# Turning the q and k of two head pairs in one DMA transfer, with v on GpSimd's queue

## The chip, the cores and the metric

The kernel runs on one core of a Trainium2 chip. The time is device time in microseconds for one execution, the median of several runs. A profiled execution gives the busy times, waits and DMA packets that are read here. Its engines are called PE (TensorE, the matrix engine; PEld are its weight loads), DVE (VectorE), ACT (ScalarE), POOL (GpSimd) and SP (SyncE, which computes nothing here and only issues DMAs). SPq in a row means SP's queue.

## The reference

Attention with a softmax that has one extra term in its denominator, and then a feed-forward layer with mish:

```python
batch, n_heads, seq, head_dim = (8, 12, 448, 64)      # q, k, v, float32
scores = scale * np.matmul(q, k.transpose(0, 1, 3, 2))
m = np.max(scores, axis=-1, keepdims=True)
e = np.exp(scores - m)
attn = e / (np.sum(e, axis=-1, keepdims=True) + np.exp(-m) + 1e-09)
x = np.matmul(attn, v)          # then heads side by side: 3584 x 768
h = x @ w_in                    # 768 x 2048
g = h * np.tanh(np.log1p(np.exp(np.minimum(h, 20.0))))   # (h itself over 20)
out = g @ w_out                 # 2048 x 768
```

## The kernel before

**Tiling.** A head pair is two heads of one batch. There are 48 of them, six per batch, and a unit is three pairs, so there are 16 units with attention, numbered from 0. The first six pairs (units 0 and 1) run in an opening of their own. From unit 4 on (`GROUP_FROM = 12`, called grouped) all units have one shape, and that is where the change lies. "The sixth unit" is unit 5, with pairs 15, 16 and 17. The instructions run on each engine in the order in which the code writes them.

**One unit u.** It works on pairs p0, p0 + 1, p0 + 2, and nxt = p0 + 3 is the first pair of the next unit. It has two halves.

The attention half has 12 steps n. In each step ACT takes the exponentials of one score tile (L330), PE makes further scores (L293, L296, L301), DVE finds their maxima (L319), and PE fills in pieces of the second feed-forward product of an earlier batch (L511) and the weighted sums of the unit before (`av_pair`, L403). Between them stand the loads and casts of the next unit's pairs: at n = 0, 3 and 6 one pair is loaded, q, k and v in three DMAs on SP's queue (L148), and at n = 3 and 6 the pair that was loaded one slot earlier is cast to bf16 by GpSimd (q on L192 or L194, k on L198, v on L178). The third pair is cast at the start of the other half.

The feed-forward half has eight columns f = 0 to 7 of the first product with mish (`mm1_mish`, L422 on PE and L450 on ACT). In it the attention weights of the unit's three pairs are normalised (`normalise`, L366 on DVE for two pairs and L364 on GpSimd for the third), and each pair's weights are turned by one DMA transpose from SP (L370, `eT<-en`). At f = 7 stand the first scores of the next unit, which need the turned q and k of pair nxt.

**How q and k come to be turned.** Scores need q and k with the head dimension on the partitions. Two ways are in use. `transpose_pair` does it on PE: four transposes each for q and k (L215) into PSUM at f = 1, 3 or 5, and then `evac_qk` copies the result out, q scaled on DVE (L255) and k on ACT (L263). `turn_by_dma` does it by DMA transposes from SP's queue (L229, `qkT<-q_bf` and `qkT<-k_bf`), one for q and one for k. Which pairs go which way is in `TURN_BY_DMA`: of unit 5 and later the first pair of each unit (15, 18, and so on to 45), and pair 46. The first pair's turn is issued after step n = 8, and that of pair 46 after step 11. For a pair turned by DMA the scale is multiplied in when q is cast.

After either way, `rest_of` copies on GpSimd the columns of q that make up the last score tile (L237, L238). For pairs turned by DMA it stands at f = 3, ahead of GpSimd's share of the normalising.

**What orders the work.** SP's queue is served in order, and a DMA that waits for its data holds up all that stand behind it: loads, turns, eT transposes and stores (L476) share it. GpSimd also works in order. Its own DMA queue carries the weight loads (L174) until unit 4 and nothing afterwards.

Of the kernel before, what the change touches and what calls it, by code (L numbers as in the profile page):

```python
# [10 lines left out]
BF16 = mybir.dt.bfloat16  # L11
# [4 lines left out]
UNIT_PAIRS = 3  # L16
# [3 lines left out]
def kernel(  # L20
# [9 lines left out]
    nc = tc.nc  # L30

    B, H, S, D = q.shape
# [3 lines left out]
    NT = 4  # L36
    SP_ = S // NT
# [10 lines left out]
    N_PAIRS = B * HP  # L48
# [4 lines left out]
    def pool(name, bufs, space=None):  # L53
        if space is None:
            return ctx.enter_context(tc.tile_pool(name=name, bufs=bufs))
        return ctx.enter_context(tc.tile_pool(name=name, bufs=bufs, space=space))

    PS = bass.MemoryType.PSUM
    singles = pool("singles", 1)
    ld_pool = pool("ld", 4)  # L60
    bf_pool = pool("bf", 6)
    qk_pool = pool("qk", 3)
    st_pool = pool("st", 5)
    eT_pool = pool("eT", 3)
    xT_pool = pool("xT", 2)
# [16 lines left out]
    def banks_apart():  # L82
# [16 lines left out]
    w_in_sb = singles.tile([128, DM_T, d_ff], BF16)  # L99
    w_out_sb = singles.tile([128, FF_T, d_model], BF16)  # L100

    N_EN = 4
    en_bufs = [
        singles.tile([128, NT, NTILE, 128], BF16, tag=f"en{i}", name=f"en{i}")
        for i in range(N_EN)
    ]
# [4 lines left out]

    GROUP_FROM = 2 * HP
    ONE_COPY = range(1, HP + UNIT_PAIRS)
    TURN_BY_DMA = tuple(p for p in range(5 * UNIT_PAIRS, N_PAIRS) if p % UNIT_PAIRS == 0 or p == N_PAIRS - UNIT_PAIRS + 1)
    SCALED_IN_CAST = (*ONE_COPY, *TURN_BY_DMA)
    q_rests = [
        singles.tile([128, 2, 64], BF16, tag=f"qr{i}", name=f"qr{i}") for i in range(UNIT_PAIRS)
# [4 lines left out]
    loaded, casted, qkT, att, xT, gT, o_sbs, stats = {}, {}, {}, {}, {}, {}, {}, {}  # L122
# [16 lines left out]
    def load_pair(p, which="qkv"):  # L139
        if p >= N_PAIRS:  # L140
            return
        b, h0 = p // HP, (p % HP) * 2
        tiles = loaded.setdefault(p, [])
        for nm, src in (("q", q), ("k", k), ("v", v)):
            if nm not in which:
                continue
            t = ld_pool.tile([SP_, 2, NT * D], FP32, tag=f"{nm}_f", name=f"{nm}_f")
            nc.sync.dma_start(  # L148
                out=t, in_=src[b, h0 : h0 + 2].rearrange("h (p t) d -> p h (t d)", t=NT)
            )  # L150
            tiles.append(t)
# [28 lines left out]
    def cast_pair(p, with_v=True):  # L180
        if p >= N_PAIRS:
            return
        q_f, k_f = loaded[p][:2]
        q_bf = bf_pool.tile([SP_, NT, 2, D], BF16, tag="q_bf", name="q_bf")
        k_bf = bf_pool.tile([SP_, NT, 2, D], BF16, tag="k_bf", name="k_bf")
        v_bf = bf_pool.tile([SP_, 2, NT * D], BF16, tag="v_bf", name="v_bf", bufs=9)
        by_t = "p h (t d) -> p t h d"
        cast_q, cast_k = nc.gpsimd.tensor_copy, nc.gpsimd.tensor_copy
        if p == 0:
            cast_q, cast_k = nc.vector.tensor_copy, nc.scalar.copy  # L190
        if p not in SCALED_IN_CAST:
            cast_q(out=q_bf, in_=q_f.rearrange(by_t, t=NT))  # L192
        else:
            nc.gpsimd.tensor_scalar(  # L194
                out=q_bf, in0=q_f.rearrange(by_t, t=NT),
                scalar1=SCALE, scalar2=1.0, op0=ALU.mult, op1=ALU.mult,
            )
        cast_k(out=k_bf, in_=k_f.rearrange(by_t, t=NT))  # L198
        casted[p] = (q_bf, k_bf, v_bf)
        if with_v:  # L200
            cast_v(p)
# [20 lines left out]
            by_s = ps[:, :].bitcast(BF16).rearrange("p (s n) -> p s n", s=2)[:, :, 0:S]  # L222
        qkT[p] = (by_s, own)

    def turn_by_dma(p):
        qk = qk_pool.tile([128, 2, S], BF16, tag="qkT", name="qkT")
        pair = qk[:, 0, :], qk[:, 1, :]
        for dst, src in zip(pair, casted[p]):
            nc.sync.dma_start_transpose(  # L229
                out=dst.rearrange("c (t q) -> c t q", q=SP_),  # L230
                in_=src.rearrange("q t h d -> q (t h d)"),
            )
        qkT[p] = pair

    def rest_of(p):
        qT, q_rest = qkT[p][0], q_rests[p % UNIT_PAIRS]
# [3 lines left out]
    def evac_qk(p, act=False):  # L240
        if p >= N_PAIRS:
            return
        by_s, own = qkT[p]
        mo_free.extend(own)
        qk = qk_pool.tile([128, 2, S], BF16, tag="qkT", name="qkT")
        qT, kT = qkT[p] = qk[:, 0, :], qk[:, 1, :]
        if p in ONE_COPY:
            copy = nc.scalar.copy if act else nc.vector.tensor_copy
            copy(out=qk, in_=by_s)
            return  # L250
        q_ps, k_ps = by_s
        if act:
            nc.scalar.mul(qT, q_ps[:, 0:S], SCALE)
        else:
            nc.vector.tensor_scalar(  # L255
                out=qT, in0=q_ps[:, 0:S], scalar1=SCALE, scalar2=None, op0=ALU.mult
            )
        if p >= GROUP_FROM:
            rest_of(p)
        if p == 0 or own and not act:  # L260
            nc.vector.tensor_copy(out=kT, in_=k_ps[:, 0:S])
        else:
            nc.scalar.copy(kT, k_ps[:, 0:S])  # L263
# [10 lines left out]
    def scores(idx):  # L274

        p, s = divmod(idx, STEPS)
        if s == 0:
# [4 lines left out]
            att[p] = {nm: t[:, at, :] for nm, t in stats.items()}  # L282
            att[p].update(en=en_bufs[p % N_EN], whole=dict(stats))
        st = att[p]
# [303 lines left out]
    BY_POOL = 3  # L588
    LEAD = UNIT_PAIRS + 1
    LOAD_AT = (0, 3, 6)  # L590
    TURN_AFTER = (8, 11)
    LAST_AV_AT = 9
    HEAD = HP

# [63 lines left out]
    for u in range(UNITS_PER_B, N_UNITS + 2 * UNITS_PER_B):  # L658
# [5 lines left out]
        p0 = u * UNIT_PAIRS  # L664
        nxt = p0 + UNIT_PAIRS
# [5 lines left out]
        for n in range(steps):  # L671
            pi, s = divmod(n, STEPS)
            p, idx = p0 + pi, p0 * STEPS + n
            late_tp = u == UNITS_PER_B and n == STEPS
            if late_tp:
                transpose_pair(p0 + 2)
            exps(idx)
            if grouped:
                flush_late()
                for what, arg in (GROUPED_LATE_AV if u == LATE_AV else GROUPED)[n]:  # L680
                    if what == "fill":
                        for _ in range(min(arg, len(filler))):
                            fn, w = filler.popleft()
                            fn()
                            done += w
                    elif what in ("av0", "av1"):
                        bank = sc_banks[int(what[2])][0]
                        av_pair(p0 - UNIT_PAIRS + arg, bank=bank)
                    else:
                        flush_late()  # L690
                        for i in arg:
                            scores(p0 * STEPS + i)
                if n in LOAD_AT:
                    at = p0 + LOAD_AT.index(n)
                    if u > first_mm2:
                        load_pair(at + LEAD - 1)
                        if n:
                            cast_pair(at + LEAD - 2)
                    elif n < LOAD_AT[-1]:
                        load_pair(at + LEAD)  # L700
                        cast_pair(at + LEAD - 1)
                if u - UNITS_PER_B < len(W_AT):
                    load_w(W_AT[u - UNITS_PER_B].get(n, 0))
                if n in TURN_AFTER and nxt + TURN_AFTER.index(n) in TURN_BY_DMA:
                    turn_by_dma(nxt + TURN_AFTER.index(n))
                continue
            if late_tp:
                evac_qk(p0 + 2, act=True)
            if u == UNITS_PER_B + 1:
                for i, part in enumerate(TURN_AT[1].get(n, [])):  # L710
                    turn_on_pe(*part)
                    if n == 0:
                        mm1_ahead(0, FIRST_AHEAD[i])
            flush_late()
            acc += weight[n]
            want = int(total * acc / sum(weight) + 1e-6)
            while done < want:
                fn, w = filler.popleft()
                fn()
                done += w  # L720
            scores_ahead(end)
            if n in LOAD_AT:
                load_pair(p0 + LOAD_AT.index(n) + LEAD)
                cast_pair(p0 + LOAD_AT.index(n) + LEAD - 1)
            if u - UNITS_PER_B < len(AV_AT):
                early = AV_AT[u - UNITS_PER_B]
                if n in early:
                    av_pair(early[n], act=early[n] in AV_BY_ACT)
                if u == UNITS_PER_B:
                    for part in TURN_AT[0].get(n, []):  # L730
                        turn_on_pe(*part, act=part in TURN_BY_ACT)
            elif u == N_UNITS and n == LAST_AV_AT:
                for i in range(UNIT_PAIRS):
                    av_pair(p0 - UNIT_PAIRS + i, bank=sc_banks[i][0])
            if u - UNITS_PER_B < len(W_AT):
                load_w(W_AT[u - UNITS_PER_B].get(n, 0))
# [9 lines left out]
        for f in range(FF_U):  # L746
# [3 lines left out]
            if moe:  # L750
                first = to_group and nxt == GROUP_FROM
                bank, ff = sc_banks[0][0] if f == 1 else None, w * FF_U + f
                if to_group:
                    at = (FIRST_MISH_BANK if first else MISH_BANK)[f]
# [68 lines left out]
```

## Time and profile before

| | |
|---|---|
| median of 3 runs | 463.99 us (462.11 to 465.33) |
| the profiled execution | 462.06 us, of which the span from its first to its last instruction is 460.3 us |
| granted PE clock over the span | 0.993 |
| busy PE, DVE, ACT, POOL | 430.8, 342.3, 343.3, 186.6 us |
| DMA issues for q, k, v | 48 each, 224 KB each, on SP |
| DMA transposes on SP | 43 of eT, 12 of q, 12 of k |

A row of a timeline gives the start in us from the span's start, the duration in us, the engine, line and operation, what it writes and reads, how many instructions were merged into the row, and in brackets how long the engine had been idle before and what ended that. In a row of a group of instructions, the counts and the durations in ns (smallest, median, largest) stand together. Durations on SP are those of the issue; the landing of the data is told apart.

### The profile page before, as it was taken

Reading aid. Unit: us, or ns where it says so; the run is one execution under the profiler, and the core shown is the slowest. Engines: PE = TensorE matmul, PEld = TensorE weight load, DVE = VectorE, ACT = ScalarE, POOL = GpSimd, SP = SyncE. Lnnn points to the kernel's source line nnn. Section 1 sums busy time; section 2 is a strip of 40 time slices with the busy share of each in tenths; the row PEclk is TensorE's granted clock in tenths of the full one; section 3 lists DMA queues with packets and bytes.
Section 4 is the critical chain, followed back from the end, with each engine's and each line's share of the span. In section 5 each row is a group of like instructions: output and inputs, shape, how many; then the busy total and the mean of one; then the engine's idle time right before and its main releaser. Section 6 shows DMA issues by size and latency. Waiting matters only on the chain.

```text
span 460.3 us, 8676 instructions
## 1 busy us (share of the span) xinstructions
PE 430.8 (94%) x2952; PEld 229.0 (50%) x2952; DVE 342.3 (74%) x718; ACT 343.3 (75%) x906; POOL 186.6 (41%) x352
## 2 busy tenths in 40 slices
PE   4586798899998999999999999999999989999997
PEld 2243445444444554545455555545454545555565
DVE  4899968879796988889787988889887969421121
ACT  5998988989795969788897969696988879211300
POOL 4666839254418172625444271707254450000000
PEclk9997999999999999999999999999999999999999
DMA  8999999999999999999999999999999996950213
GB/s 218 221 194 229 272 190 229 207 210 197 215 254 240 223 221 227 252 216 264 204 248 215 253 197 244 199 234 249 209 243 201 258 198 142 182 127 0 70 34 104
DMA packets 213900, 93.11 MB, mean 202 GB/s; under 512 B 170592, under 2 KB 210400, under 8 KB 213856
## 3 DMA queue, kind: packets, MB, share of 16 engines
q1 hardware_dynamic: 206272, 86.22, 89.2%
q0 software_dynamic: 7488, 6.29, 9.4%
q8 instruction: 23, 0.38, 0.3%
q14 instruction: 21, 0.17, 0.1%
q10 hardware_dynamic: 96, 0.05, 0.0%
HBM read 45.61 MB, written 11.01 MB: 123 GB/s over the span
## 4 chain that ended last, share of the span: by engine, by line
PE 72%; DMA 8%; ACT 6%; DVE 6%; issue 2%; SPq 2%; POOL 1%; POOLq 0%; DVEq 0%
PE mo L511 29%; PE mo L422 21%; PE b L403 6%; PE b L422 6%; ACT en L330 5%; DVE negm L319 4%; PE b L293 3%; DMA k_f<-in_k_dram 3%; DMA q_f<-in_q_dram 2%; PE sc L293 2%; DMA eT<-en 2%; DMA qkT<-k_bf 1%; SPq L370 1%; PE mo L301 1%; PE sc L215 1%
## 5 line engine op out<-in xcount | busy, mean ns | idle before, releaser
L511 PE MATMUL mo<-w_out_sb,gT 128*128 128x384 bf16 (+1 forms) x896 | 141.5, 304 | 0.9 <-DVE o_sb L498 0.7
L422 PE MATMUL mo<-xT,w_in_sb 128*128 128x448 bf16 x600 | 124.3, 353 | 0.8 <-DVE xT L412 0.3
L511 PEld LDWEIGHTS <-gT 128*128 128x128 bf16 x896 | 80.2, 98 | 58.8 <-issue 20.2
L422 PEld LDWEIGHTS <-w_in_sb 128*128 128x128 bf16 x768 | 72.2, 98 | 66.6 <-issue 7.2
L450 ACT ACTIVATE gT<-mo 128x448 bf16<-128x448 f32 x98 | 53.0, 544 | 70.0 <-PE mo L422 69.5
L330 ACT ACTIVATE en<-sc,negm 128x448 bf16<-128x448 f32 x156 | 97.8, 641 | 7.6 <-DVE negm L319 6.3
L319 DVE TENSOR_REDUCE negm<-b 128x1 f32<-128x448 f32 x144 | 79.8, 617 | 19.4 <-PE b L296 19.4
L330 ACT ACTIVATE en<-b,negm 128x448 bf16<-128x448 f32 x144 | 89.7, 652 | 0.8 <-DVE negm L319 0.8
L319 DVE TENSOR_REDUCE negm<-sc 128x2 f32<-128x896 f32 x84 | 84.2, 1016 | 6.3 <-PE sc L296 4.0
L364 POOL TENSOR_SCALAR en<-en,rden 128x448 bf16<-128x448 bf16 x109 | 67.5, 640 | 24.3 <-DVE rden L358 17.4
L366 DVE TENSOR_SCALAR en<-en,rden 128x448 bf16<-128x448 bf16 x227 | 76.3, 405 | 0.7
L498 DVE COPY o_sb<-mo 128x384 f32<-128x384 f32 (+1 forms) x64 | 32.2, 504 | 48.5 <-PE mo L511 44.7
L194 POOL TENSOR_SCALAR q_bf<-q_f 112x512 bf16<-112x512 f32 x20 | 12.5, 624 | 106.5 <-DMA q_f<-in_q_dram 106.4
L293 PE MATMUL sc<-qkT 64*128 64x448 bf16 x72 | 28.5, 402 | 10.9 <-ACT en L330 8.7
L403 PE MATMUL b<-eT,v_bf 112*64 112x448 bf16 x304 | 35.8, 358 | 1.4 <-DMA eT<-en 1.4
L422 PE MATMUL b<-xT,w_in_sb 128*128 128x448 bf16 x162 | 35.2, 352 | 0.0
L178 POOL CAST v_bf<-v_f 112x512 bf16<-112x512 f32 x48 | 30.3, 631 | 7.8 <-DMA v_f<-in_v_dram 7.1
L198 POOL CAST k_bf<-k_f 112x512 bf16<-112x512 f32 x47 | 29.8, 634 | 7.7 <-DMA k_f<-in_k_dram 6.9
L330 ACT ACTIVATION_READ_ACCUMULATOR en<-sc,negm 128x1 f32 x156 | 32.8, 211 | 0.0
L330 ACT ACTIVATION_READ_ACCUMULATOR en<-b,negm 128x1 f32 x144 | 32.6, 226 | 0.0
L192 POOL CAST q_bf<-q_f 112x512 bf16<-112x512 f32 x27 | 17.5, 648 | 28.6 <-DMA q_f<-in_q_dram 28.6
L403 PEld LDWEIGHTS <-v_bf 112*64 112x64 bf16 x384 | 19.1, 110 | 20.0 <-issue 10.5
(70 smaller groups left out, 482.9 us busy)
## 6 DMA issues: line engine op xcount, KB each, us to landing
q_f<-in_q_dram SPq DMA_DIRECT2D x48, 224.0 KB, 5.2
k_f<-in_k_dram SPq DMA_DIRECT2D x48, 224.0 KB, 5.4
v_f<-in_v_dram SPq DMA_DIRECT2D x48, 224.0 KB, 5.5
w_in_sb<-in_moe_w_in_dram POOLq DMA_DIRECT2D x12, 256.0 KB, 6.2
w_out_sb<-in_moe_w_out_dram POOLq DMA_DIRECT2D x8, 384.0 KB, 8.4
out_dram<-o_sb SPq DMA_DIRECT2D x7, 336.0 KB, 4.3
out_dram<-o_sb SPq DMA_DIRECT2D x8, 288.0 KB, 3.7
out_dram<-o_sb SPq DMA_DIRECT2D x8, 240.0 KB, 4.9
```

What stands on the lines that cost most here:

```text
L178: nc.gpsimd.tensor_copy(out=casted[p][2], in_=loaded.pop(p)[2])
L198: cast_k(out=k_bf, in_=k_f.rearrange(by_t, t=NT))
L293: nc.tensor.matmul(sc[0][:, 0:S], lhsT=qT[0:64, qa : qa + 128], rhs=kA, start=True, stop=True)
L319: nc.vector.tensor_reduce(out=negm, in_=scored, axis=AX.X, op=ALU.max, negate=True)
L330: nc.scalar.activation(out=st["en"][:, :, c, 0:SP_], in_=sc[bk][:, 0:S].rearrange("q (j c) -> q j c", j=NT), func=AF.Exp, bias=st["negm"][ ...
L364: nc.gpsimd.tensor_scalar(scalar2=1.0, op0=ALU.mult, op1=ALU.mult, **args)
L366: nc.vector.tensor_scalar(scalar2=None, op0=ALU.mult, **args)
L403: nc.tensor.matmul(av[h * 64 : (h + 1) * 64, 0:S], lhsT=v_bf[:, h, j * D : (j + 1) * D], rhs=e_h, start=(j == 0), stop=(j == NT - 1),)
L422: nc.tensor.matmul(h_ps[:, 0:S], lhsT=w_in_sb[:, dm, ff * 128 : (ff + 1) * 128], rhs=xT[b][:, dm, :], start=(dm == 0), stop=(dm == DM_T - 1),)
L450: nc.scalar.activation(out=gT[b][:, ff, :], in_=h_ps[:, 0:S], func=AF.Mish)
L498: nc.vector.tensor_copy(out=o_sb[:, cols], in_=st["o"][:, 0:n_cols])
L511: nc.tensor.matmul(st["o"][:, 0:n_cols], lhsT=src[:, ff, c0 : c0 + 128], rhs=w_out_sb[:, ff, cols], start=(ff == 0), stop=(ff == FF_T - 1),)
```

## The change

The buffers of the cast q and k become one tile for six pairs, and those of the turned q and k one tile for three, so that a single transfer can read and write two pairs. From unit 5 on, the first two pairs of each unit are turned by one DMA transpose of 112 partitions by 2048 columns, issued after step 11. The third pair is turned on PE as before. For pairs after 15, v is loaded by a DMA that GpSimd issues, in the same place of the code where SP issued it.

```diff
-    bf_pool = pool("bf", 6)
-    qk_pool = pool("qk", 3)
+    bf_pool = pool("bf", 9)
...
+    N_CAST = 2 * UNIT_PAIRS
+    qk_bf = singles.tile([SP_, N_CAST, 2, NT, 2, D], BF16)
+    qk_all = singles.tile([128, UNIT_PAIRS, 2, S], BF16)
...
-    TURN_BY_DMA = tuple(p for p in range(5 * UNIT_PAIRS, N_PAIRS) if p % UNIT_PAIRS == 0 or p == N_PAIRS - UNIT_PAIRS + 1)
+    TURN_BY_DMA = tuple(
+        p for p in range(GROUP_FROM + UNIT_PAIRS, N_PAIRS) if p % UNIT_PAIRS < 2
+    )
...
-            nc.sync.dma_start(
+            queue = nc.gpsimd if nm == "v" and p > GROUP_FROM + UNIT_PAIRS else nc.sync
+            queue.dma_start(
...
-        q_bf = bf_pool.tile([SP_, NT, 2, D], BF16, tag="q_bf", name="q_bf")
-        k_bf = bf_pool.tile([SP_, NT, 2, D], BF16, tag="k_bf", name="k_bf")
-        v_bf = bf_pool.tile([SP_, 2, NT * D], BF16, tag="v_bf", name="v_bf", bufs=9)
+        q_bf, k_bf = (qk_bf[:, p % N_CAST, i] for i in range(2))
+        v_bf = bf_pool.tile([SP_, 2, NT * D], BF16, tag="v_bf", name="v_bf")
...
-    def turn_by_dma(p):
-        qk = qk_pool.tile([128, 2, S], BF16, tag="qkT", name="qkT")
-        pair = qk[:, 0, :], qk[:, 1, :]
-        for dst, src in zip(pair, casted[p]):
-            nc.sync.dma_start_transpose(
-                out=dst.rearrange("c (t q) -> c t q", q=SP_),
-                in_=src.rearrange("q t h d -> q (t h d)"),
-            )
-        qkT[p] = pair
+    def turn_by_dma(p0, n):
+
+        to, at = p0 % UNIT_PAIRS, p0 % N_CAST
+        nc.sync.dma_start_transpose(
+            out=qk_all[:, to : to + n].rearrange("c a s (t q) -> c (a s t) q", q=SP_),
+            in_=qk_bf[:, at : at + n].rearrange("q a s t h d -> q (a s t h d)"),
+        )
+        for p in range(p0, p0 + n):
+            qkT[p] = tuple(qk_all[:, p % UNIT_PAIRS, i, :] for i in range(2))
...
-        qk = qk_pool.tile([128, 2, S], BF16, tag="qkT", name="qkT")
+        qk = qk_all[:, p % UNIT_PAIRS]
...
-    TURN_AFTER = (8, 11)
+    TURN_AFTER = 11
...
-                if n in TURN_AFTER and nxt + TURN_AFTER.index(n) in TURN_BY_DMA:
-                    turn_by_dma(nxt + TURN_AFTER.index(n))
+                if n == TURN_AFTER and nxt in TURN_BY_DMA:
+                    turn_by_dma(nxt, 2)
```

## The prediction

> **What bounds the kernel now.** I read the busy shares of the page first, then the busy times stage by stage, then the timeline of SP's queue against that of GpSimd. The busy time and share of each engine, from the page:
>
> ```profile
> PE 430.8 (94%) x2952; PEld 229.0 (50%) x2952; DVE 342.3 (74%) x718; ACT 343.3 (75%) x906; POOL 186.6 (41%) x352
> ```
>
> The table by stage has one steady unit per row (span, then busy PE, PEld, DVE, ACT, POOL, granted clock, DMA share, GB/s); the last row is the last unit with attention.
>
> ```profile
> 211.28:236.38 25.10, 25.10 (x174) 13.12 (x173) 21.54 (x46) 21.16 (x57) 12.03 (x25) 1.00 1.11 238
> 236.38:261.49 25.11, 25.11 (x175) 13.12 (x173) 19.98 (x45) 21.16 (x57) 11.16 (x22) 1.00 1.08 227
> 361.90:388.00 26.10, 24.73 (x167) 12.64 (x165) 21.48 (x45) 20.85 (x56) 10.40 (x20) 1.00 1.01 194
> ```
>
> In a steady unit TensorE has no idle time: 25.10 us of 25.10. DVE and ACT have 3.5 to 5 us of room, POOL 13. So TensorE work taken away should pay in full, as long as nothing else is nearly as long. SP's queue is. This is one unit of it, from one set of attention transposes to the next:
>
> ```profile
> 215.82 13.55 SPq L370 DMA_TRANSPOSE eT<-en  x3
> 229.42 0.57 SPq L148 DMA_DIRECT2D q_f<-in_q_dram  x1
> 230.04 0.47 SPq L148 DMA_DIRECT2D k_f<-in_k_dram  x1
> 230.56 0.46 SPq L148 DMA_DIRECT2D v_f<-in_v_dram  x1
> 231.06 0.46 SPq L148 DMA_DIRECT2D q_f<-in_q_dram  x1
> 231.56 0.46 SPq L148 DMA_DIRECT2D k_f<-in_k_dram  x1
> ...
> 236.96 1.20 SPq L229 DMA_TRANSPOSE qkT<-q_bf  x1
> 238.26 1.21 SPq L229 DMA_TRANSPOSE qkT<-k_bf  x1
> 239.56 1.00 SPq L476 DMA_DIRECT2D out_dram<-o_sb  x2
> 240.66 14.21 SPq L370 DMA_TRANSPOSE eT<-en  x3
> ...
> 266.15 13.14 SPq L370 DMA_TRANSPOSE eT<-en  x3
> ```
>
> The entries stand nearly back to back. The first and the last set of three that matter, with nine units between them:
>
> ```profile
> 115.37 13.50 SPq L370 DMA_TRANSPOSE eT<-en  x3
> ...
> 342.33 14.30 SPq L370 DMA_TRANSPOSE eT<-en  x3
> ```
>
> They end at 128.87 and at 356.63: 227.76/9 = 25.31 us per unit. So two chains of nearly one length run side by side, TensorE's at 25.1 and SP's at 25.3, and what the change does to each has to be worked out apart.
>
> **TensorE's part.** What one pair's turn costs there is seen on the chain that ended last, in the eight transposes between two groups of feed-forward matmuls:
>
> ```profile
> 239.79 1.14 PE b L422 x6
> 240.92 0.20 PE sc L215 x4
> 241.12 0.20 PE b L215 x4
> 241.32 2.27 PE mo L422 x12
> ```
>
> 0.40 us a pair. Twelve pairs are turned by DMA now (15, 18 and so on to 45, and 46), 22 afterwards, so ten leave TensorE: 10 x 0.40 = **4.0 us** if TensorE alone decides. With each go one DVE and one ACT instruction, which lay beside TensorE's work and had room (worth nothing alone):
>
> ```profile
> L255 DVE TENSOR_SCALAR qkT<-sc x27: 374/384/392, 63.2 to 369.6; 128x448 bf16<-128x448 bf16 x27
> L263 ACT COPY qkT<-b x24: 524/532/563, 89.7 to 369.2; 128x448 bf16<-128x448 bf16 x24
> ```
>
> There is one stall besides that the DMA side owns, in the last attention unit, where the first weighted sum waits for its transposed weights:
>
> ```profile
> 370.19 0.36 PE L293 MATMUL b<-qkT 64*128 64x448 bf16 x1
> 376.33 0.95 PE L403 MATMUL b<-eT,v_bf 112*64 112x448 bf16 x8 [1.37 <-DMA eT<-en]
> 368.87 7.42 DMA eT<-en
> ```
>
> Between the scores at 370.19 and that sum lie 376.33 - 1.37 - 370.19 = 4.77 us of TensorE work.
>
> **SP's part, price of the turn.** The only transposes the trace shows are of 28 blocks of 128 columns (eT) and of 4 (one q or k):
>
> ```profile
> L370 SPq DMA_TRANSPOSE eT<-en x43: 4127/4314/6272, 19.8 to 400.3; - x43
> L229 SPq DMA_TRANSPOSE qkT<-q_bf x12: 1184/1196/1919, 109.3 to 366.3; - x12
> eT<-en SPq DMA_TRANSPOSE x43, 6.7
> ```
>
> The new one has 16. A line through both gives (4.31 - 1.20)/24 = 0.13 us a block over a fixed 0.68: **2.75 us**. By eT's price per block alone it is 2.46, by four issues of today 4.80. I take the line, since both rows lie on one engine and one form. It replaces two issues of 1.2. From issue to landing an eT takes 6.7 in the median, 2.4 after its issue; with 1.5 to 2.4 behind 2.75 the new turn lands some 4.6 us after it starts.
>
> **What it waits for.** This is the real change of order. Today's turn needs only the first pair's casts and goes out as soon as SP gets to it. The joint one needs the k cast of the *second* pair, and behind it on SP stand the three eT issues, on which the weighted sums wait, and behind those the next unit's loads. So SP's chain becomes: end of the eT issues, loads of the first pair, loads of the second, landing, two casts, turn, eT. GpSimd's second pair:
>
> ```profile
> 236.27 0.62 POOL L192 CAST q_bf<-q_f 112x512 bf16<-112x512 f32 x1 [0.42 <-DMA q_f<-in_q_dram]
> 236.93 0.61 POOL L198 CAST k_bf<-k_f 112x512 bf16<-112x512 f32 x1
> ...
> 263.75 0.62 POOL L198 CAST k_bf<-k_f 112x512 bf16<-112x512 f32 x1
> ...
> 288.10 0.62 POOL L198 CAST k_bf<-k_f 112x512 bf16<-112x512 f32 x1
> ...
> 365.68 0.89 POOL L198 CAST k_bf<-k_f 112x512 bf16<-112x512 f32 x1
> ```
>
> The k casts end at 237.54, 264.37, 288.72 and 366.57; the eT issues before them ended at 229.37, 254.87, 279.29 and 356.63. The latency is 8.17, 9.50, 9.43 and 9.94 us, on average 9.3. The sixth unit, with four stores between its loads, is longer:
>
> ```profile
> 139.05 0.62 POOL L198 CAST k_bf<-k_f 112x512 bf16<-112x512 f32 x1
> ```
>
> 139.67 - 128.87 = 10.8, so 1.5 more.
>
> GpSimd waits for the turn as well. It copies a rest of q for each turned pair, now for two of them, and only then normalises its share of the third pair:
>
> ```profile
> 242.55 0.23 POOL L237 COPY qr<-qkT 64x64 bf16<-64x64 bf16 x1 [0.30 <-DMA qkT<-q_bf]
> 243.77 4.33 POOL L364 TENSOR_SCALAR en<-en,rden 128x448 bf16<-128x448 bf16 x7 [0.71 <-DMA out_dram<-o_sb]
> ```
>
> From the k cast: turn landed 4.65, four copies 1.0, normalising 4.33, so 10.0. The third eT issue starts 2.85 + 2 x 4.35 = 11.5 after the cast, so these 1.5 us cover it. The stores that stand behind today's turn (239.56) come out ahead of the joint one, in its wait, and cost nothing there.
>
> **v through GpSimd.** 32 loads leave SP, three per unit, but only one of them (the first pair's v) stands ahead of the second pair's k. It is worth 0.5 us if only its issue on SP counts (0.46 and a gap), and 1.0 if its bytes do too (229 KB at the 232 GB/s of the two units above). The two v's that GpSimd issues earliest move into its idle stretch beside the eT issues. If they still get in the way of the same loads, the gain is nothing. I take 0.8, nearer to the upper end, because an eT issue and its data leave the queue at a steady pace that is set by SP's issue: latency **8.5**. On GpSimd a load costs about what a weight load does:
>
> ```profile
> L174 POOL DMA_DIRECT2D w_in_sb<-in_moe_w_in_dram x12: 713/752/895, 14.6 to 73.7; - x12
> ```
>
> 32 x 0.75 = 24 us over ten units, under POOL's 13 idle us in each. The third pair's v is issued right before the second pair's casts, where POOL stood waiting 0.42 us for q; without that cover its 0.33 us of excess would go into the turn. The Trainium skill (SBUF — State Buffer, section "SBUF: two separate sides") says that a DMA issued from GpSimd can't write its descriptors while DVE runs in a two-port mode, and gives 620 ns turned into 3100; by an estimate from that page the third v would hold the turn back 2.5 us a unit. No run here shows it. I leave it out of the sum.
>
> **The sum.** SP's new spacing: 8.5 + 2.75 + 0.1 of gaps + 13.7 (mean of 13.50, 13.55, 14.21, 13.14 and 14.30) = **25.05 us**, against 25.31 now and TensorE's 24.7 after its cut. SP's chain decides. The fifth unit's eT end stays at 128.87, because there SP has time to spare:
>
> ```profile
> 109.85 0.62 POOL L198 CAST k_bf<-k_f 112x512 bf16<-112x512 f32 x1 [2.08 <-DMA k_f<-in_k_dram]
> 110.61 1.21 SPq L229 DMA_TRANSPOSE qkT<-k_bf  x1
> ```
>
> A joint turn from 110.5 ends by 113.3, and the eT issues start at 115.37. Ten units on, the second pair's k is cast at 128.87 + 9 x 25.05 + 1.5 + 8.5 = 364.3. The turn lands at 368.9, so the scores go 1.2 us before today's 370.19; TensorE reaches the first weighted sum at 373.7, and its eT lands at 364.3 + 2.85 + 6.7 = 373.9, against 376.33: **2.5 us saved**. After that the tail is as it was. The profiled execution took 462.06 us (span 460.3 and 1.8 around it), 1.9 under the median shown of 463.99, at its runs' low end. So 459.6 beside the profiled one, **461.5 us** on the scale of the median. It is a small gain: of some 5.4 us that TensorE gives up, half goes to the wait for the second pair.
>
> **Rivals.**
>
> *TensorE alone decides.* If SP's spacing falls to 24.7 (the v's hidden wholly, worth 1.0 or a little more, and eT at 13.5), all 4.0 us and the 1.37 us stall come back: 463.99 - 5.4 = 458.6. For it: v lands early and three issues leave SP. Against it: the chain has no slack left to lose.
>
> *The second pair is late (the other side).* The v's go through the same DMA engines, so the loads before the turn come no earlier: latency 9.3, spacing 25.85, k cast at 128.87 + 9 x 25.85 + 1.5 + 9.3 = 372.3, weighted sum at 381.9: 5.5 us later, 469.5. It begins to cost above a spacing of (376.33 - 9.55 - 128.87 - 1.5 - 8.5)/9 = 25.3. For it: a DMA share above 1 in every unit. Against it: SP's rows, where the gaps between loads are SP's own. The Trainium skill (DMA: Bandwidth & Descriptors, "Issuing engines are not separate DMA queues") is on this side: issuing from several engines saves only the sequencer's time. That the page's rule holds for a queue whose transposes are paced by their issue no run here shows yet.
>
> *The joint turn is not cheaper.* At 4.80 the spacing is 27.1, the k cast at 382.8, the sum at 394.4: 18 us later, 482. For it: the number of blocks is the same. Against it: eT moves 28 blocks in 4.31.
>
> **How the numbers follow.** SP's chain near today's length, within 1% (what a measurement of this kernel can about tell from no change, 4.6 us): 0.45. TensorE alone: 0.28, all of it faster by over 1%. Late second pair by enough to be over 1%: 0.20. Dear turn: 0.07. So faster 0.28, same 0.45, slower 0.27. The range goes from TensorE alone less a run's spread (458.6 - 1.6, as 462.11 to 465.33 spread about the median) to the late pair with 1 us on top: 457.0 to 470.5. The forecast's own case is 459.4 to 468.6. A tenth of a us in the spacing is worth 1 us at the end, since ten units repeat it; that is why the range is wide for so small an edit.
>
> **What would show it.** Right: TensorE's transposes of L215 in the middle of the feed-forward half gone; turns of 2.5 to 3 us, one per unit; eT's first issue 2.8 us behind a POOL cast of k; sets of eT spaced 24.8 to 25.3; TensorE's idle time before L293 of some tenths a unit. Wrong: turns over 4 us; eT issues over 4.6 us with v in flight; GpSimd stuck in an issue of v for over 1 us, or waiting for v rather than q; no idle time on TensorE at all, which would be the first rival.

## The result, and the profile after

| | before | after |
|---|---|---|
| median | 464.17 us (462.11 to 465.33) | 485.15 us (482.43 to 490.37) |
| profiled execution, its span | 462.06, 460.3 us | 482.43, 480.6 us |
| granted PE clock over the span | 0.993 | 0.977 |

The changed kernel is **slower by 4.4%**: ratio 1.0437, 95% interval 1.0373 to 1.0502. The forecast was 461.5 us, and 485 lies outside the range. Ratios here leave disturbed runs out, so one can differ from what the medians beside it would give.

The busy times of the page, after:

```profile
PE 432.5 (90%) x2872; PEld 226.8 (47%) x2872; DVE 342.4 (71%) x708; ACT 339.3 (71%) x896; POOL 206.2 (43%) x384
```

TensorE has 80 matmuls fewer, and the span is 20 us longer. Its share went from 94% to 90%: it waits now. For what, the groups of the page say, first of before and then of after (busy and mean ns, then idle time ahead of the group and what ended it):

```profile
L403 PE MATMUL b<-eT,v_bf 112*64 112x448 bf16 x304 | 35.8, 358 | 1.4 <-DMA eT<-en 1.4
```

```profile
L408 PE MATMUL b<-eT,v_bf 112*64 112x448 bf16 x304 | 37.0, 367 | 17.6 <-DMA eT<-en 16.3
```

The weighted sums waited 1.4 us for turned attention weights, and wait 17.6 now, 16.3 of it for the landing of eT. The chain that ended last says the same, before and then after:

```profile
PE 72%; DMA 8%; ACT 6%; DVE 6%; issue 2%; SPq 2%; POOL 1%; POOLq 0%; DVEq 0%
```

```profile
PE 54%; DMA 20%; DVE 10%; ACT 9%; issue 3%; POOL 1%; SPq 1%; DVEq 0%; POOLq 0%; ACTq 0%
```

The timeline of SP after, with its turns (L233) and sets of eT (L375). The first row is the fifth unit's set, the last the set nine units on:

```profile
116.70 17.20 SPq L375 DMA_TRANSPOSE eT<-en  x3
...
197.44 15.47 SPq L375 DMA_TRANSPOSE eT<-en  x3
...
222.52 1.53 SPq L233 DMA_TRANSPOSE qk_all<-qk_bf  x1
224.16 17.10 SPq L375 DMA_TRANSPOSE eT<-en  x3
...
249.59 3.46 SPq L233 DMA_TRANSPOSE qk_all<-qk_bf  x1
253.15 17.45 SPq L375 DMA_TRANSPOSE eT<-en  x3
...
361.75 14.77 SPq L375 DMA_TRANSPOSE eT<-en  x3
```

The fifth unit's set ends at 133.91 (before 128.87), the one nine units later at 376.52 (356.63). The 20.3 us of span are therefore 5.0 us by the end of the fifth unit, 242.61 - 227.76 = 14.85 us in the nine units (26.96 against 25.31 each), and 0.4 in the tail. A set of eT took 13.1 to 14.3 us before; here 14.7 to 17.5.

GpSimd's timeline shows what runs beside these sets. This issue of two v's falls into the set that began at 197.44:

```profile
205.79 1.38 POOL L154 DMA_DIRECT2D v_f<-in_v_dram  x2
```

And the table by stretch, for three sets of before and then three of after (span, busy PE, PEld, DVE, ACT, POOL, granted clock, DMA share, GB/s):

```profile
215.82:229.37 13.55, 13.55 (x95) 6.87 (x94) 10.81 (x24) 10.47 (x27) 7.61 (x16) 1.00 1.16 204
240.66:254.87 14.21, 14.21 (x103) 7.27 (x101) 10.31 (x24) 10.86 (x28) 6.41 (x15) 1.00 1.12 206
266.15:279.29 13.14, 13.14 (x91) 6.62 (x88) 10.54 (x23) 10.09 (x26) 7.40 (x16) 1.00 1.14 199
```

```profile
197.44:212.91 15.47, 15.47 (x104) 7.41 (x102) 12.19 (x26) 12.34 (x33) 7.42 (x16) 1.00 1.11 203
224.16:241.25 17.09, 12.94 (x85) 6.13 (x83) 11.86 (x25) 11.63 (x32) 7.63 (x17) 0.95 1.14 185
253.15:270.60 17.45, 17.32 (x115) 8.29 (x112) 13.11 (x25) 14.32 (x41) 8.89 (x18) 1.00 1.09 180
```

With two v's on top the DMA engines move no more per microsecond: 180 to 203 GB/s in these three sets, against 199 to 206, and 180 to 221 in all nine, against 193 to 223. What looked like an idle stretch of GpSimd's queue had no room in the DMA engines behind all queues: the sets took the added bytes only by growing longer. The rate alone does not tell this. Between the sets the kernel before moves more, 246 to 275 GB/s, as here:

```profile
229.37:240.66 11.29, 11.29 (x80) 6.08 (x77) 10.05 (x22) 10.69 (x31) 4.87 (x8) 1.00 1.05 260
```

Why a stretch of eT transposes passes fewer bytes per microsecond than one of loads, stores and a turn isn't shown by these runs.

### The profile page after: what moved, and what is told of

It is laid out like the page before. It is cut to its first block, busy times and chain, and to the rows that moved or that the text cites. A ratio compares the mean times of both kernels' runs of the same rounds, so it can differ in the third digit from the quotient of the medians.

```text
span 480.6 us, 8480 instructions
## 1 busy us (share of the span) xinstructions
PE 432.5 (90%) x2872; PEld 226.8 (47%) x2872; DVE 342.4 (71%) x708; ACT 339.3 (71%) x896; POOL 206.2 (43%) x384
## 4 chain that ended last, share of the span: by engine, by line
PE 54%; DMA 20%; DVE 10%; ACT 9%; issue 3%; POOL 1%; SPq 1%; DVEq 0%; POOLq 0%; ACTq 0%
PE mo L516 19%; PE mo L427 18%; DMA eT<-en 17%; ACT en L335 7%; DVE negm L324 6%; PE b L427 5%; PE b L408 4%; PE sc L298 2%; PE b L298 2%; DVE en L371 2%; DMA k_f<-in_k_dram 2%; DMA q_f<-in_q_dram 1%; PE mo L386 1%; ACT qk_all L254 1%; PE mo L306 1%
## 5 line engine op out<-in xcount | busy, mean ns | idle before, releaser
L516 PE MATMUL mo<-w_out_sb,gT 128*128 128x384 bf16 (+1 forms) x896 | 143.3, 306 | 0.8 <-DVE o_sb L503 0.7
L516 PEld LDWEIGHTS <-gT 128*128 128x128 bf16 x896 | 81.2, 99 | 60.2 <-issue 21.8
L371 DVE TENSOR_SCALAR en<-en,rden 128x448 bf16<-128x448 bf16 x227 | 74.5, 399 | 0.7
L199 POOL TENSOR_SCALAR qk_bf<-q_f 112x512 bf16<-112x512 f32 x30 | 18.9, 632 | 121.8 <-DMA q_f<-in_q_dram 121.6
L408 PE MATMUL b<-eT,v_bf 112*64 112x448 bf16 x304 | 37.0, 367 | 17.6 <-DMA eT<-en 16.3
L298 PE MATMUL sc<-qk_all 64*128 64x448 bf16 x72 | 28.7, 404 | 11.3 <-ACT en L335 10.4
L417 DVE CAST xT<-b 128x448 bf16<-128x448 f32 x38 | 23.5, 619 | 19.4 <-PE b L408 19.2
L335 ACT ACTIVATE en<-mo,negm 128x448 bf16<-128x448 f32 x36 | 23.1, 642 | 14.5 <-DVE negm L324 14.5
L203 POOL CAST qk_bf<-k_f 112x512 bf16<-112x512 f32 x47 | 29.3, 623 | 5.8 <-DMA k_f<-in_k_dram 5.5
L335 ACT ACTIVATION_READ_ACCUMULATOR en<-b,negm 128x1 f32 x144 | 31.4, 218 | 0.0
```

The source lines that it names most:

```text
L298: nc.tensor.matmul(sc[0][:, 0:S], lhsT=qT[0:64, qa : qa + 128], rhs=kA, start=True, stop=True)
L335: nc.scalar.activation(out=st["en"][:, :, c, 0:SP_], in_=sc[bk][:, 0:S].rearrange("q (j c) -> q j c", j=NT), func=AF.Exp, bias=st["negm"][ ...
L371: nc.vector.tensor_scalar(scalar2=None, op0=ALU.mult, **args)
L408: nc.tensor.matmul(av[h * 64 : (h + 1) * 64, 0:S], lhsT=v_bf[:, h, j * D : (j + 1) * D], rhs=e_h, start=(j == 0), stop=(j == NT - 1),)
L417: copy(out=xT[b][:, hp, :], in_=av[:, 0:S])
L516: nc.tensor.matmul(st["o"][:, 0:n_cols], lhsT=src[:, ff, c0 : c0 + 128], rhs=w_out_sb[:, ff, cols], start=(ff == 0), stop=(ff == FF_T - 1),)
```

## The experiments

Four readings were to be told apart: v beside the eT sets; GpSimd as the issuer; the joint turn's place behind the second pair; and the bytes that a unit sends through the DMA engines. For the last, the table by stretch is read over the nine units from the fifth unit's eT end: the stretch divided by 9 is the spacing, and GB/s times spacing the bytes of a unit. Before, that is 25.31 us and 5.82 MB:

```profile
128.87:356.63 227.76, 226.34 (x1551) 117.13 (x1549) 191.01 (x401) 190.50 (x505) 101.93 (x198) 1.00 1.11 230
```

and after 26.96 us and 6.07 MB:

```profile
133.91:376.52 242.61, 224.18 (x1450) 113.62 (x1451) 187.71 (x385) 183.26 (x484) 118.65 (x225) 0.98 1.07 225
```

The DMA share adds up the time that packets took, so that it can pass 1.

### The parts of the change by themselves

The joint turn alone, v on SP:

```diff
-            queue = nc.gpsimd if nm == "v" and p > GROUP_FROM + UNIT_PAIRS else nc.sync
+            queue = nc.sync
```

> The joint turn of two pairs alone; all loads of v stay on SP. Theory A (the loads of v that run beside the eT transposes through a second queue lengthen those, and the joint turn is harmless): the sets of three eT issues go back from 15.5 to 17.5 us to 13.1 to 14.3, the joint turn keeps its 1.5 to 2.5 us, the first weighted sum no longer waits, and the time is 457 to 463 us. Theory B (the joint turn's wait for the second pair's k is what makes the chain of SP long): most of the 21 us stays, 475 us or more.

Measured 472.00 us, ratio 1.0187 (1.0121 to 1.0252), spacing 26.33:

```profile
131.21:368.16 236.95, 223.42 (x1475) 112.86 (x1472) 190.04 (x391) 186.45 (x494) 102.61 (x198) 1.00 1.08 230
```

That lies between what either theory alone would give. The sets of eT are back at 13.7 on average, but the turn starts 9.9 us after the set before it. So the joint turn by itself costs some 9 us, and v on another queue the other 12.

v alone on GpSimd, turns as before:

```diff
-            nc.sync.dma_start(
+            queue = nc.gpsimd if nm == "v" and p > GROUP_FROM + UNIT_PAIRS else nc.sync
+            queue.dma_start(
```

> The turns as before (one pair, two transfers), v on GpSimd's queue from pair 16 on. Theory A: the second and third eT of each unit land 2 to 4 us later, as after the whole change; the three issues that SP is rid of give back 1.5 us of it per unit, so 475 to 487 us. Theory B: within 1% of before, 460 to 468 us.

Ratio 1.029 (1.0185 to 1.0394). Its runs lie from 473.12 to 488.29, so only the sign is used: taking v off SP is a loss without the joint turn, too.

The whole change with v on ScalarE's queue (`nc.gpsimd` becomes `nc.scalar` in that line):

> The whole change, with v issued from ACT's queue in the same places of the code in the place of GpSimd's. ACT works in order, so these issues come at the steps where they are written and the first two may start later than on GpSimd. Theory A1 (any second queue beside the eT transposes lengthens them): eT sets of 15 us or more wherever a v is in flight with them, 475 to 487 us, unless ACT's order keeps the two apart. Theory A2 (something of GpSimd's queue alone): eT sets of 13.1 to 14.3 with v in flight, 458 to 466 us. Theory B: 475 us or more with eT sets of 13 to 14.

483.99 us, ratio 1.0445 (1.0397 to 1.0493): the same as the change itself. Its sets of eT average 15.2 us (15.5 after, 13.7 before). So GpSimd as the issuer is not the cause: v's that run beside the eT sets cost the same from ScalarE's queue.

Only the third pair's v on GpSimd (`and p % UNIT_PAIRS == 2`), which is issued beside the loads, and then only the second pair's (`== 1`), which is issued beside the eT set:

> The whole change, but only the third pair's v of each unit goes through GpSimd; that one is issued just before the second pair's casts and lands ahead of the eT issues. The other two v's are back on SP. Theory A: the eT sets are 13.1 to 14.3 us, and the time is 457 to 464 us. If each v on GpSimd costs alike wherever it falls, a third of the loss stays: about 471 us. Theory B: 475 us or more.

> The whole change, but only the second pair's v of each unit goes through GpSimd: one v beside the eT transposes in the place of two (two gave sets of 15.7 us on average, none 13.7 to 13.9). If the DMA engines are full in these sets and a v costs its bytes there, one gives 14.6 to 15.0 and the time is 473 to 481 us. If two queues in use cost by themselves, the sets are as long as with two, 15.5 us or more, and the time is that of the whole change.

The third alone: 472.84 us, ratio 1.0176 (1.0101 to 1.0251), sets of 13.9, no worse than the joint turn with no v moved. The second alone: 479.95, ratio 1.0357 (1.0317 to 1.0396), sets of 14.7. With none, one and two v's beside it a set takes 13.7, 14.7 and 15.5 us. So a v (224 KB, 229,376 bytes) costs **0.9 us** there, about its own bytes at the 230 GB/s of a unit (1.0). One v costs half of what two do, so it isn't the use of a second queue as such.

### Where v could go instead

v on SP, but behind all q and k of the unit, so that nothing of it stands ahead of the turn (its casts follow at f = 6):

```diff
-                        load_pair(at + LEAD - 1)
+                        load_pair(at + LEAD - 1, "qk")
+                        if n == LOAD_AT[-1]:
+                            for i in range(UNIT_PAIRS):
+                                load_pair(nxt + i, "v")
```

> The joint turn with all loads on SP, but v of the three pairs issued behind the q and k of all three, and cast by GpSimd at the seventh feed-forward column, when it has nothing else to do. If the joint turn lost because loads of v stood ahead of the second pair's k (its cast came 9.8 us after the eT issues with v between, 8.4 with v gone), the latency is 8.0 to 8.8 us, the eT sets stay at 13.1 to 14.3, SP's spacing is 24.7 to 25.2 and the time 458 to 464 us. If the wait for a second pair costs whatever stands ahead, the latency stays above 9.3 and the time is 469 us or more.

474.82 us, ratio 1.0264 (1.0206 to 1.0322): a miss. The turn starts 9.0 us after the set (9.9 with v ahead), but its issue now takes 3.4 us in the mean (2.6), and the spacing is 26.19. The same order with a transfer for each pair, the first after n = 8 and the second after n = 11:

> As the run with v behind q and k on SP, and the two pairs turned by a transfer each, the first after step 8 and the second after step 11. Only the second then stands behind the second pair's k, at about 1.7 us in the place of 2.75. If SP's chain through that k decides, the spacing is 1 us less than with one transfer, TensorE decides, and the time is 457 to 461 us. If it is the number of transfers that counts, this is 1 to 2 us a unit slower than one transfer: 469 us or more.

471.06, ratio 1.0188 (1.0135 to 1.024): a miss again. And v on GpSimd, issued beside the loads and not beside the eT set:

> The joint turn with all v's on GpSimd's queue, but issued behind the first pair's casts (two) and the second pair's casts (one), so that they run beside the loads and not beside the eT transposes. The v's are cast at the seventh feed-forward column. If only the place beside the transposes is harmful, the sets are 13.1 to 14.3 us, the latency 8.4 to 9.5, and the time 460 to 470 us. If GpSimd's queue is harmful anywhere, sets or latencies are longer than with all loads on SP and the time is 475 us or more.

476.42, ratio 1.0265 (1.02 to 1.033). The sets (14.2 in the mean) and the wait (8.8) came out as for "only the place beside the transposes is harmful", the time as for the other side. Three orders, none faster. What they share is that one pair more, 229 KB, is turned by DMA, and behind a second pair's k. The run of two transfers:

```profile
132.01:365.94 233.93, 221.50 (x1468) 112.06 (x1468) 183.58 (x389) 185.74 (x492) 101.65 (x198) 1.00 1.12 233
```

6.06 MB at 233 GB/s are its 25.99 us.

### The bytes

The kernel before with one load of 224 KB more in each unit, into a tile that nobody reads:

```diff
+                if n == 9 and u > first_mm2 and nxt < N_PAIRS:
+                    nc.scalar.dma_start(out=spare[0], in_=q[b_, h_ : h_ + 2]...)
```

> The kernel before, with one plain load more in each unit from the sixth on: 224 KB of q, read a second time into a tile that nobody uses, issued by ScalarE's queue after step n = 9. SP's issues, their order and every wait of the turn are as before. Theory C (the 16 DMA engines are full: a unit's time is its bytes at about 226 GB/s, as 5.73 MB in 25.31 us before): 5.96 MB at 226 makes 26.3 us of a unit, and the time 470 to 474 us. Rival (the chain of SP's issues and the wait for a k cast sets the spacing, and the DMA engines have room): the spacing stays at 25.3 to 25.6 us, the time at 461 to 466 us.

468.59 us, ratio 1.0128 (1.0067 to 1.019), spacing 26.10:

```profile
127.29:362.21 234.92, 226.96 (x1548) 116.62 (x1547) 191.41 (x401) 191.83 (x508) 101.68 (x198) 1.00 1.12 232
```

No instruction of the computation was touched and SP issues what it did, but 6.06 MB take 0.79 us longer than 5.82. The spacing is near the 26.3 of the bytes and above the 25.6 of the rival; the time lies between the two ranges, 1.4 us under that of the bytes. So bytes cost time in the kernel before, but less than in proportion. The other way round, the joint turn of the first run with halved v:

```diff
+            n_h = 1 if nm == "v" and p > GROUP_FROM + UNIT_PAIRS else 2
...
-                out=t, in_=src[b, h0 : h0 + 2]...
+                out=t[:, 0:n_h], in_=src[b, h0 : h0 + n_h]...
```

> The joint turn with v on SP, and from the sixth unit on only the first head's half of each v is loaded (112 KB in place of 224); the second head takes the first head's v, so the result is not the reference's. The number of issues is the same. Theory C: 5.62 MB of a unit at 226 GB/s are 24.8 us, less than TensorE's 25.1 before less 0.40, so that TensorE decides again and the time is 458 to 463 us. Rival (SP's issues and the wait for the second pair's k set the spacing, whatever the bytes): the latency falls by some 0.4 us only, the spacing is 25.9 us, and the time 467 to 471 us.

470.33 us, ratio 1.0124 (1.0072 to 1.0175), spacing 25.81: here **the rival was right**, and the bytes alone are not the whole cause.

```profile
131.90:364.18 232.28, 222.37 (x1472) 112.87 (x1471) 186.16 (x389) 185.55 (x493) 108.72 (x225) 1.00 1.05 221
```

The DMA engines pass only 221 GB/s. Two terms of the order hold this run: the wait for the second pair's k (9.7 us after the eT set) and, behind it, turn and eT set (2.0 and 13.9). So the reading from here on is two limits close together, where one taken away shows the other. With both taken away (v behind q and k, and halved):

> The joint turn with v on SP behind all q and k of a unit, as in the run of that order, and in it from the sixth unit on only the first head's half of each v is loaded (112 KB in place of 224); the second head takes the first head's v, so the result is not the reference's. Theory D, two limits close together: the joint turn's place behind the second pair's loads (25.8 us of a unit with the halved v between the loads) and what the DMA engines pass (6.05 MB of a unit at 230 to 233 GB/s, 26.0 to 26.3 us). Here both are taken away: 8.5 of latency, 2 to 2.5 of the turn, 0.1 and 13.8 of the eT set are 24.4 to 24.9 us, 5.7 MB at 232 GB/s are 24.6, and TensorE's 24.7 to 25.0 decides: 456 to 462 us. Rival (the DMA engines are no limit: the issue of the joint turn is long, 3.3 us as in that run, and so 8.5, 3.3, 0.1 and 13.7 make 25.6 whatever the bytes): 466 us or more.

465.51 us, ratio 1.0033 (1.0003 to 1.0064), spacing 25.49. The same halving that bought 1.7 us with v between q and k (472.00 to 470.33, which the intervals don't tell from nothing) buys 9.3 us in this order (474.82 to 465.51), and the turn falls from 3.4 to 2.1 us in the mean. But 465.5 is 3.5 over the upper end of what both limits taken away were to give. What remains is seen on TensorE, in the timeline of the sixth unit:

```profile
149.18 0.36 PE L304 MATMUL b<-qk_all 64*128 64x448 bf16 x1 [2.31 <-DMA qk_all<-qk_bf]
```

The first scores wait for the joint transfer. With a transfer for each pair, otherwise the same:

> As the run with v behind all q and k and halved (from the sixth unit on only the first head's half of each v is loaded and the second head takes it, so the result is not the reference's), but each pair turned in a transfer of its own, the first as soon as its k is cast. If what that run stayed above its forecast are waits of the scores for the joint transfer (2.3 us in the first changed unit, 1.6 in another): these go, TensorE's 24.8 to 25.0 us decide, 459 to 463 us. If they are not (the pairs turned by DMA cost another engine or wait as much as TensorE saves): 464 to 468 us.

461.49 us, **ratio 0.9949** (0.9913 to 0.9985), spacing 25.03:

```profile
132.19:357.47 225.28, 222.11 (x1476) 113.39 (x1473) 183.12 (x391) 185.99 (x496) 106.33 (x225) 1.00 1.10 228
```

TensorE's busy time is 222.11/9 = 24.68 us a unit, the 24.7 of the prediction, and all but 0.35 us of the spacing: now it sets the time. Against the same order with whole v (471.06) the halving is worth 9.6 us. The control, halved v in the kernel before:

> The kernel before with halved v from the sixth unit on (only the first head's half is loaded, the second head takes it, so the result is not the reference's); one pair turned by DMA as before. If TensorE alone sets the 25.3 us of a unit there, the bytes taken away buy nothing: spacing 25.1 to 25.3, 461 to 464 us. If the DMA engines hold it back too (5.82 MB at 230 GB/s are 25.3): a lower spacing, 24.9 or less, and 456 to 460 us.

464.01 us, ratio 1.0 (0.9957 to 1.0043). The kernel before gains nothing by fewer bytes: TensorE, busy for 225.46 of 226.12 us in the nine units of this run, sets its time. The drop of 9 us comes only with the extra turned pair.

Last, no pair turned by DMA:

```diff
-    TURN_BY_DMA = tuple(p for p in range(5 * UNIT_PAIRS, N_PAIRS) if p % UNIT_PAIRS == 0 or p == N_PAIRS - UNIT_PAIRS + 1)
+    TURN_BY_DMA = ()
```

> The kernel before with no pair turned by DMA: all q and k pass through TensorE. Theory C: 229 KB less in a unit, so that the DMA engines need 24.4 us of it, while TensorE gets 0.40 us more and needs 25.5; twelve units by 0.40 are 4.8 us, less 1.37 us of the stall in the last attention unit: 465 to 468 us. Rival (one pair's turn costs the chain of DMAs more than TensorE even in the kernel before, so that it was already past the best number of turned pairs): 463 us or less.

466.77 us, ratio 1.0067 (1.0027 to 1.0108), as expected from TensorE's 0.40 us a pair. One pair a unit by DMA is the best of none, one and two in the orders tried here. No run that computes the whole result beats the kernel before.

## Why the prediction was wrong, step by step

- **TensorE's saving: right.** 0.40 us a pair; both directions of it were seen (the run with none turned by DMA, and 24.68 us a unit in the run of 461.49).
- **The wait for the second pair's k: right, with its size.** The turn after starts 8.6 us behind the eT set in the mean of nine units (8.5 was taken). That v's departure caused the shortening is borne out by the joint turn alone, which shows 9.9.
- **The joint turn's price: right, a little dear.** 1.3 to 3.5 us, 2.1 in the mean, against 2.75. Four issues' worth, the third rival, is out.
- **"eT set unchanged at 13.7": the step that failed.** It took 15.5 us in the mean. The sum took 13.7 over from the kernel before without a reason of its own. The nearest to one is the sentence by which it chose 0.8 us for the v's, "an eT issue and its data leave the queue at a steady pace that is set by SP's issue", and that is wrong: the v's went into stretches in which the DMA engines had no room, and each pushed the eT's back by 0.9 us. The rule of the Trainium skill that the prediction weighed (DMA: Bandwidth & Descriptors, section "Issuing engines are not separate DMA queues") was right here, with 483.99 us from ScalarE's queue beside 485.15 from GpSimd's. The prediction drew from it only that the loads come no earlier. Here it costs more than that, because the v's run beside transposes that are waited for.
- **The gap of 0.1 between turn and eT set: 0.7.** Most of it comes from two units, with 2.7 and 1.8 us; in the first of them SP's queue waits for attention weights that DVE is still normalising (280.04 to 282.18). That they are late because TensorE had waited for eT before is likely and not shown. So the terms are 8.6 + 2.1 + 0.7 + 15.5 = 26.9 us, against 8.5 + 2.75 + 0.1 + 13.7 = 25.05.
- **The fifth unit's end, "stays at 128.87": wrong.** The first v's on GpSimd run beside that unit's eT set already (17.20 us, before 13.50), and with ScalarE's queue it took 17.0. With v on SP it took 13.8 in the joint turn alone, but 16.6 and 15.2 in the two runs with v behind q and k, whose loads are issued as there up to that unit. So how much of these 5.0 us is v's isn't shown. With them the miss is complete: 9 x (26.96 - 25.05) + 5.0 = 22.2 of the 22.8 us between 459.6, forecast for a run like the profiled one, and 482.43.
- **A resource that the sum left out.** One more pair through the DMA engines is 0.24 MB of a unit, 0.8 us by the load added to the kernel before, to save 0.40 us of TensorE. At 230 GB/s the kernel before stood 1% under the highest rate that any run here passed over nine units (233). The rival "late second pair" came nearest in its mechanism: its side, its reason (a DMA share over 1), but 16 us short, since it put v's bytes ahead of the loads and not into the eT sets. The 482 of the rival "the joint turn is not cheaper" is nearest in number, by luck: it needs turns of 4.80 us, and they took 2.1.
- **The signs.** "eT issues over 4.6 us with v in flight" was named as a sign of wrong, and came: the largest is 8.4 us, in the set at 253.15 (5.5 before in the grouped units, 6.3 in the opening). The rule of the Trainium skill that the prediction left out of its sum (SBUF — State Buffer, section "SBUF: two separate sides"), of GpSimd's descriptors held back by DVE, does not show in the issues: GpSimd's issue of a v takes 662 to 730 ns.

```profile
L154 POOL DMA_DIRECT2D v_f<-in_v_dram x32: 662/712/730, 97.9 to 382.0; - x32
L375 SPq DMA_TRANSPOSE eT<-en x43: 4125/4525/8385, 19.9 to 418.9; - x43
```

**What stays open.** Why the joint turn with v between the loads waits 9.7 us with halved v as against 9.9 with whole ones isn't settled: 112 KB less ahead of the second pair's k should have bought 0.5 us. Nor is it settled why v on GpSimd beside the loads took 476 us at a spacing of 26.12, under the 26.33 of the joint turn alone: its fifth unit ended 7.2 us later than before, and no run shows why. And the run of v on GpSimd alone spreads too widely to be split up.

## What to carry to other kernels

Before a transfer is moved into an "idle stretch", ask what the DMA engines do there and not only the queue that issues there. Neither an idle queue nor a GB/s below the best shows room: the eT sets ran at 193 to 223 GB/s, under the 246 to 275 between them, and yet each v added there delayed them by about its own bytes, from either of the two queues tried. One run with a single transfer moved tells. When two chains tie, price a trade in both: here 0.40 us of TensorE was bought with 0.8 us of DMA. And when taking away one suspected limit changes nothing, take away both before giving the theory up: the halving of v was worth 0 us in the kernel before, 1.7 in the joint turn, and 9.3 and 9.6 with v behind q and k.

## What the runs showed of the hardware that was not expected

A stall of 2 to 3 us can cost TensorE more than itself. In the timeline after, TensorE's sums resume at 239.40 and at 273.57:

```profile
239.40 1.52 PE L408 MATMUL b<-eT,v_bf 112*64 112x448 bf16 x8 [3.25 <-DMA eT<-en]
```

```profile
273.57 1.18 PE L408 MATMUL b<-eT,v_bf 112*64 112x448 bf16 x6 [3.10 <-DMA eT<-en]
```

and the granted clock in the 3.4 us behind each is half:

```profile
239.60:243.00 3.40, 3.40 (x15) 1.22 (x11) 0.91 (x2) 0.00 (x0) 0.00 (x0) 0.50 1.24 246
273.80:277.20 3.40, 3.40 (x21) 2.18 (x18) 0.89 (x2) 0.00 (x0) 2.80 (x5) 0.50 1.08 358
```

By an estimate from the half clock, that is another 1.7 us lost each time, which no sum of waits contains. The Trainium skill (TensorE: Matmul & The Clock Gate, section "What's actually happening") puts the half rate down to an idle window of about 3.4 us. Here shorter stalls were enough. That of 2.31 us at 149.18, in the run with v behind q and k and halved, is followed by 3.4 us at half clock, from 149.9 on:

```profile
149.90:153.30 3.40, 3.40 (x12) 1.43 (x11) 2.89 (x5) 1.01 (x2) 3.26 (x7) 0.51 1.08 211
```

After the change a stall of 2.20 us was enough, too:

```profile
136.01 0.95 PE L408 MATMUL b<-eT,v_bf 112*64 112x448 bf16 x8 [2.20 <-DMA eT<-en]
```

```profile
137.30:140.70 3.40, 3.40 (x11) 1.35 (x10) 3.33 (x11) 0.87 (x2) 2.50 (x4) 0.51 0.96 290
```

The joint turn alone had a stall of 2.21 us, with the full clock in the 4 us from there on:

```profile
145.01 0.37 PE L220 MATMUL sc<-ident,qk_bf 112*128 112x112 bf16 x4 [2.21 <-POOL qk_bf L197]
```

```profile
145.00:149.00 4.00, 3.55 (x26) 1.67 (x27) 1.67 (x4) 1.08 (x2) 2.52 (x7) 1.00 1.10 171
```

So the length of the stall alone doesn't decide; what does isn't shown here. The three stalls of the change shown above all lie in the nine units, whose mean granted clock is 0.98 against 1.00 before.
